# Laying K, V, dK and dV out in DRAM so that each partition moves 8 KB in one run instead of 4 KB twice

## The chip, the cores and the metric

The kernel runs on one core of one Trainium2 chip. The metric is the time of one execution on the device in microseconds. Executions of the kernel before in one round agree within 0.3 to 1% (691.9 to 694.2 us in one, 690.6 to 697.3 in another), and a ratio is called faster or slower only beyond 2%. The rearrangement of the arrays on the host is not in the time.

## The reference

Attention with grouped heads, forward and backward, in bf16. There are 32 batches; in each, 32 query heads of 4 rows share 4 K/V heads of 2048 rows, with 128 columns.

```python
def _fwd_reference(q, k, v):               # q (32, 32, 4, 128); k, v (32, 4, 2048, 128)
    k = jnp.repeat(k, rep, axis=1)         # rep = 8
    v = jnp.repeat(v, rep, axis=1)
    p = _softmax(jnp.einsum("bhqd,bhkd->bhqk", q, k) * D ** -0.5, axis=-1)
    return jnp.einsum("bhqk,bhkd->bhqd", p, v)

def reference(q, k, v, grad_out):          # returns out, dq, dk, dv
    _out, _vjp = jax.vjp(_f, q, k, v)
    return (_out, *_vjp(grad_out))
```

The 128 query rows of a batch fill the 128 partitions. K, V, dK and dV of a batch are 2 MB each, 8 MB together. The other four arrays come to 128 KB per batch.

## The kernel before

K and V come in as pairs of heads, 1 MB per transfer. On each of the 128 partitions lie 16 rows of one head (4 KB, contiguous in DRAM) and 16 rows of the other (4 KB, 512 KB away). dK and dV leave in the same form. A batch therefore has eight transfers of 1 MB on the sync engine's queue (SP) and four of 32 KB on GpSimd's (POOL). TensorE transposes K and V (L372 in the profile), transposes the softmax and its gradient (L431), and does the products (L383, L442, L477). ScalarE (ACT) and VectorE (DVE) empty PSUM. The order of all instructions over the batches is fixed by a table.

```python
CAP = dict(q=4, k=8, v=4, ..., out=6)      # buffers; a K or V buffer holds one pair of heads
...
pairs = lambda t: t.rearrange("b (g h) (p c) d -> b g p h (c d)", c=C, h=2)
k_r, v_r, dk_r, dv_r = pairs(k), pairs(v), pairs(out_2), pairs(out_3)
...
elif name in ("LK", "LV"):                                          # L358
    g, = arg
    p_, src = (k_pool, k_r) if name == "LK" else (v_pool, v_r)
    x = p_.tile([P, 2, C, D], BF16, name="k_sb" if name == "LK" else "v_sb")
    whole = x[:].rearrange("p h c d -> p h (c d)")
    for h in range(2) if b == 0 else [slice(0, 2)]:
        nc.sync.dma_start(out=whole[:, h], in_=src[b, g][:, h])
...
elif name in ("DVs", "DKs"):                                        # L492
    g, = arg
    nc.sync.dma_start(out=(dv_r if name == "DVs" else dk_r)[b, g],
                      in_=t[name[:2], "out", g][:].rearrange("p h c d -> p h (c d)"))
```

Eight K buffers are four batches, four V buffers are two. Each 1 MB transfer has one of eight completion semaphores in turn, so at most eight are in flight.

Of the kernel before, what the change touches and what calls it, by code (L numbers as in the profile page):

```python
# [15 lines left out]
P = 128  # L16
NH = 4
# [261 lines left out]
def kernel(  # L279
# [10 lines left out]
):  # L290
    nc = tc.nc
    B, Hq, Sq, D = q.shape
    Hkv, Sk = k.shape[1], k.shape[2]
    assert D == P and Hq * Sq == P and Hkv == NH and Hq // Hkv * Sq == 32
    C = Sk // P
    QW = Sk // NQ
# [16 lines left out]
    make_identity(nc, ident[:])  # L313

    rows = lambda t: t.rearrange("b h s d -> b (h s) d")
    pairs = lambda t: t.rearrange("b (g h) (p c) d -> b g p h (c d)", c=C, h=2)
    q_r, go_r, o_r, dq_r = rows(q), rows(grad_out), rows(out_0), rows(out_1)
    k_r, v_r, dk_r, dv_r = pairs(k), pairs(v), pairs(out_2), pairs(out_3)

# [178 lines left out]
                emit(u)  # L498

_INS = ['q', 'k', 'v', 'grad_out']  # L500
_OUTS = [((32, 32, 4, 128), 'bfloat16'), ((32, 32, 4, 128), 'bfloat16'), ((32, 4, 2048, 128), 'bfloat16'), ((32, 4, 2048, 128), 'bfloat16')]

# [23 lines left out]
```

## Time and profile before

| | before |
|---|---|
| time, median | 692.5 us (691.9 to 694.2, 4 runs) |
| span of the profiled execution | 688.6 us |
| TensorE, ScalarE busy | 90%, 88% |
| packets on the main queue | 70,784 |

Lines of the page of the kernel before: the rate of the transfers in 40 slices of the span, the queues, and the chain of work that ended last.

```profile
GB/s 347 403 413 387 415 414 409 415 415 416 415 416 416 414 416 412 397 407 413 408 409 405 410 412 414 399 398 412 405 412 405 406 401 397 408 403 386 391 260 263
...
q1 hardware_dynamic: 70784, 268.45, 97.6%
q0 software_dynamic: 4096, 4.20, 1.8%
q8 instruction: 96, 1.57, 0.8%
...
DMA 55%; PE 22%; ACT 13%; issue 5%; POOL 3%; DVE 2%; SPq 0%; POOLq 0%; DVEq 0%; ACTq 0%
```

Queue q1 carries the 1 MB transfers, q0 the small ones, q8 the instructions of TensorE. The rate is about 415 GB/s until slice 16 (280 us) and about 405 after it. More than half of the chain is transfers.

The busy time of the engines in three stretches of the kernel before (columns: stretch in us, its length, then busy us and number of instructions for TensorE, its weight loads, VectorE, ScalarE and GpSimd, then granted clock, share of the transfer engines, GB/s):

```profile
100.00:270.00 170.00, 160.65 (x3237) 121.44 (x3233) 143.79 (x200) 159.04 (x242) 55.71 (x112) 1.00 1.03 415
300.00:380.00 80.00, 73.68 (x1470) 55.96 (x1467) 65.64 (x91) 72.62 (x111) 26.12 (x52) 1.00 1.02 408
400.00:600.00 200.00, 182.26 (x3626) 136.86 (x3624) 162.23 (x230) 179.46 (x274) 59.05 (x119) 1.00 1.02 406
```

TensorE is busy 94.5% of the first stretch and 91 to 92% of the others. The waits of the kernel before from 270 to 600 us (total, number, longest) say why:

```profile
PEld L372 <- DMA v_sb<-in_v_dram: 18.4, 15, 1.5
PE psum L372 <- DMA v_sb<-in_v_dram: 11.3, 14, 1.0
```

TensorE waits for V here, and for no load between 100 and 270 us. One pace follows from the starts of the exponentials: 20.3 us per batch from batch 5 to batch 12, and 21.14 from batch 14 to batch 28.

### The profile page before, as it was taken

The page shows a single profiled execution, that of the slowest core. Times are in us where ns is not written, and L with a number is a line of the kernel's source. Part 1 is how long each engine was busy: PE and PEld are TensorE (multiplying, and loading weights), DVE is VectorE, ACT ScalarE, POOL GpSimd, SP SyncE. Part 2 cuts the span into 40 slices and gives each one's busy share as a digit, 9 for nine tenths or more (in the row PEclk, how much of TensorE's full clock was granted, in tenths as well). Part 3 has the DMA queues.
Part 4 walks back from the last instruction along what each step waited for, and adds up shares of the span by engine and source line. Part 5 has one row for each costly group of instructions (what it writes and reads, how often), then busy time and mean ns, then how long its engine had stood idle before and what let it go on. Part 6 is the DMA issues. An engine that isn't in the chain of part 4 may idle for free.

```text
span 688.6 us, 28403 instructions
## 1 busy us (share of the span) xinstructions
PE 620.1 (90%) x12352; PEld 467.1 (68%) x12352; DVE 558.3 (81%) x776; ACT 604.4 (88%) x921; POOL 208.8 (30%) x426
## 2 busy tenths in 40 slices
PE   5899999999999999999999899998889998989984
PEld 4677677777677777766667666676666766766753
DVE  3788888888889888888788878787787887888885
ACT  2889999999999999998899888899888998888883
POOL 2423321333322233331233321333212333113330
PEclk9999999999999999999999999999999999999998
DMA  9999999999999999999999999999999999999967
GB/s 347 403 413 387 415 414 409 415 415 416 415 416 416 414 416 412 397 407 413 408 409 405 410 412 414 399 398 412 405 412 405 406 401 397 408 403 386 391 260 263
DMA packets 75005, 274.47 MB, mean 399 GB/s; under 512 B 6272, under 2 KB 6272, under 8 KB 74880
## 3 DMA queue, kind: packets, MB, share of 16 engines
q1 hardware_dynamic: 70784, 268.45, 97.6%
q0 software_dynamic: 4096, 4.20, 1.8%
q8 instruction: 96, 1.57, 0.8%
q14 instruction: 29, 0.24, 0.1%
HBM read 136.31 MB, written 136.31 MB: 396 GB/s over the span
## 4 chain that ended last, share of the span: by engine, by line
DMA 55%; PE 22%; ACT 13%; issue 5%; POOL 3%; DVE 2%; SPq 0%; POOLq 0%; DVEq 0%; ACTq 0%
DMA v_sb<-in_v_dram 52%; PE psum L372 10%; PE psum L477 6%; ACT dk_sb L483 4%; ACT dv_sb L483 4%; PE psum L431 3%; DMA out_dram<-dv_sb 2%; ACT e_sb L399 2%; PE psum L442 2%; ACT vt_sb L337 2%; POOL dop_sb_103 L411 1%; PE psum L383 1%; DVE kt_sb L390 1%; ACT kt_sb L337 1%; DMA go_sb<-in_grad_out_dram 1%
## 5 line engine op out<-in xcount | busy, mean ns | idle before, releaser
L483 ACT CAST dk_sb<-psum 128x1024 bf16<-128x1024 f32 x159 | 157.6, 1013 | 25.9 <-PE psum L477 24.5
L483 ACT CAST dv_sb<-psum 128x1024 bf16<-128x1024 f32 x155 | 151.7, 1022 | 13.2 <-PE psum L477 12.4
L372 PE MATMUL psum<-ident,v_sb 128*128 128x128 bf16 x2048 | 147.4, 220 | 16.8 <-DMA v_sb<-in_v_dram 15.3
L372 PEld LDWEIGHTS <-v_sb 128*128 128x128 bf16 x2048 | 117.9, 98 | 56.9 <-issue 32.8
L372 PE MATMUL psum<-ident,k_sb 128*128 128x128 bf16 x2048 | 142.4, 221 | 10.2 <-ACT dk_sb L483 10.2
L372 PEld LDWEIGHTS <-k_sb 128*128 128x128 bf16 x2048 | 121.4, 99 | 27.1 <-issue 24.3
L483 DVE CAST dv_sb<-psum 128x1024 bf16<-128x1024 f32 x101 | 122.8, 1220 | 10.8 <-PE psum L477 10.6
L483 DVE CAST dk_sb<-psum 128x1024 bf16<-128x1024 f32 x97 | 115.9, 1219 | 8.5 <-ACT kt_sb L337 4.5
L337 ACT COPY kt_sb<-psum 128x512 f32<-128x512 f32 x190 | 110.3, 595 | 6.6 <-PE psum L372 5.1
L411 POOL TENSOR_SCALAR dop_sb_103<-go_sb,rinv 32x128 bf16<-32x128 bf16 x64 | 38.5, 602 | 225.4 <-DVE rinv L404 97.3
L411 POOL TENSOR_SCALAR dop_sb_102<-go_sb,rinv 32x128 bf16<-32x128 bf16 x64 | 38.5, 602 | 212.5 <-DVE rinv L404 141.1
L463 DVE SCALAR_TENSOR_TENSOR ds_sb<-psum,delta,e_sb 128x1024 bf16<-128x1024 f32 x64 | 81.9, 1279 | 15.1 <-ACT vt_sb L337 13.5
L337 ACT COPY vt_sb<-psum 128x512 f32<-128x512 f32 x131 | 75.5, 599 | 17.6 <-PE psum L372 16.6
L340 DVE COPY vt_sb<-psum 128x1024 bf16<-128x1024 bf16 x125 | 82.9, 681 | 2.9 <-PE psum L372 2.6
L477 PEld LDWEIGHTS <-e_sb 64*128 64x128 bf16 x1024 | 50.0, 93 | 36.3 <-issue 19.6
L399 ACT ACTIVATE e_sb<-psum,m 128x1024 bf16<-128x1024 f32 x64 | 71.1, 1122 | 2.4 <-DVE kt_sb L390 2.2
L340 DVE COPY kt_sb<-psum 128x1024 bf16<-128x1024 bf16 x66 | 44.9, 685 | 18.8 <-PE psum L372 18.8
L477 PEld LDWEIGHTS <-ds_sb 64*128 64x128 bf16 x1024 | 43.3, 94 | 23.8 <-issue 8.8
L477 PE MATMUL psum<-dop_sb_103,e_sb 64*128 64x256 bf16 x512 | 45.2, 270 | 4.1 <-POOL dop_sb_103 L411 1.6
L477 PE MATMUL psum<-dop_sb_102,e_sb 64*128 64x256 bf16 x512 | 44.9, 270 | 3.2 <-ACT dv_sb L483 0.7
L390 DVE TENSOR_SCALAR_CACHE_REDUCE kt_sb<-psum 128x1024 bf16<-128x1024 f32 x32 | 39.2, 1225 | 9.6 <-issue 7.7
L390 DVE TENSOR_SCALAR_CACHE_REDUCE kt_sb<-psum,m 128x1024 bf16<-128x1024 f32 x32 | 41.1, 1284 | 6.5 <-DVE kt_sb L390 3.9
(83 smaller groups left out, 764.5 us busy)
## 6 DMA issues: line engine op xcount, KB each, us to landing
k_sb<-in_k_dram SPq DMA_DIRECT2D x62, 1024.0 KB, 18.7
v_sb<-in_v_dram SPq DMA_DIRECT2D x62, 1024.0 KB, 19.6
out_dram<-dv_sb SPq DMA_DIRECT2D x62, 1024.0 KB, 19.0
out_dram<-dk_sb SPq DMA_DIRECT2D x62, 1024.0 KB, 18.8
k_sb<-in_k_dram SPq DMA_DIRECT2D x4, 512.0 KB, 5.4
v_sb<-in_v_dram SPq DMA_DIRECT2D x4, 512.0 KB, 9.4
out_dram<-dv_sb SPq DMA_DIRECT2D x4, 512.0 KB, 7.9
out_dram<-dk_sb SPq DMA_DIRECT2D x4, 512.0 KB, 6.7
```

Source lines behind the costliest of these rows:

```text
L337: nc.scalar.copy(out=out.rearrange("p c d -> p (c d)").bitcast(FP32), in_=in_.rearrange("p c d -> p (c d)").bitcast(FP32))
L340: nc.vector.tensor_copy(out=out, in_=in_)
L372: nc.tensor.transpose(out=ps[:, j, :], in_=t[x, h][:, 8 * i + j, :], identity=ident[:])
L383: nc.tensor.matmul(t[name, i][r, QW * w:QW * w + QW], lhsT=t["qdt"][:, side, r], rhs=t[x, h, i][:, CPQ * w:CPQ * w + CPQ, :], start=True, ...
L390: nc.vector.tensor_scalar(out=spent, in0=t["S", i][:], scalar1=-scale, scalar2=t["m"][:] if i else None, op0=ALU.mult, op1=ALU.min, accum_ ...
L399: nc.scalar.activation(out=t["e"][:, 2 * QW * i:2 * QW * i + 2 * QW], in_=t["S", i][:], func=ACT.Exp, bias=t["m"][:], scale=scale, accum_o ...
L411: nc.gpsimd.tensor_scalar(out=t["dop"][r, h % 2, :], in0=t["go"][r, :], scalar1=t["rinv"][r, :], scalar2=None, op0=ALU.mult)
L431: nc.tensor.transpose(out=ps[:, j, :], in_=src[:, P * c:P * c + P], identity=ident[:])
L442: nc.tensor.matmul(t[name][r, 0:D], lhsT=t[xt, c // 8][:, c % 8, r], rhs=t[x, h][:, c, :], start=(c == 0), stop=(c == C - 1), tile_positio ...
L463: nc.vector.scalar_tensor_tensor(out=t["ds"][:, w], in0=t["DP", i][:], scalar=t["dl"][:], in1=t["e"][:, w], op0=ALU.subtract, op1=ALU.mult)
L477: nc.tensor.matmul(accs[g][:, 2 * P * j:2 * P * j + 2 * P], lhsT=t[lhs][r, P * c:P * c + P], rhs=t[rhs][r, :, :].rearrange("p h d -> p (h ...
L483: copy(out=t[name[:2], "out", g][:, :, CPQ * i:CPQ * i + CPQ, :], in_=t[name[:2], i][g][:].rearrange("p (c h d) -> p h c d", h=2, d=D))
```

## The change

The host lays K and V out as (batch, pair, partition, head, 16 rows, column) and undoes it for dK and dV, so each partition's 8 KB is one contiguous run in DRAM. The intent is half as many packets for the same bytes. No instruction of the compute engines changes.

```diff
-    Hkv, Sk = k.shape[1], k.shape[2]
+    Hkv, Sk = k.shape[1] * k.shape[3], k.shape[2] * k.shape[4]
...
-    pairs = lambda t: t.rearrange("b (g h) (p c) d -> b g p h (c d)", c=C, h=2)
+    pairs = lambda t: t.rearrange("b g p h c d -> b g p h (c d)")
...
-_OUTS = [..., ((32, 4, 2048, 128), 'bfloat16'), ((32, 4, 2048, 128), 'bfloat16')]
+_OUTS = [..., ((32, 2, 128, 2, 16, 128), 'bfloat16'), ((32, 2, 128, 2, 16, 128), 'bfloat16')]
+
+def paired(x):
+
+    return x.reshape(32, 2, 2, P, 16, P).transpose(0, 1, 3, 2, 4, 5)
+
+def unpaired(x):
+    return x.transpose(0, 1, 3, 2, 4, 5).reshape(32, NH, 16 * P, P)
...
-        a = _np.ascontiguousarray(inputs[name])
+        a = _np.ascontiguousarray(paired(_np.asarray(inputs[name])) if name in "kv" else inputs[name])
...
-    return got
+    return got[:2] + tuple(unpaired(_np.asarray(x)) for x in got[2:])
```

More of the change, by code (lines that the diff above doesn't have):

```diff
@@ L500 @@
 _INS = ['q', 'k', 'v', 'grad_out']
-_OUTS = [((32, 32, 4, 128), 'bfloat16'), ((32, 32, 4, 128), 'bfloat16'), ((32, 4, 2048, 128), 'bfloat16'), ((32, 4, 2048, 128), 'bfloat16')]
+_OUTS = [((32, 32, 4, 128), 'bfloat16'), ((32, 32, 4, 128), 'bfloat16'), ((32, 2, 128, 2, 16, 128), 'bfloat16'), ((32, 2, 128, 2, 16, 128), 'bfloat16')]
+def paired(x):
+    return x.reshape(32, 2, 2, P, 16, P).transpose(0, 1, 3, 2, 4, 5)
+def unpaired(x):
+    return x.transpose(0, 1, 3, 2, 4, 5).reshape(32, NH, 16 * P, P)
 def kernel(**inputs):
```

## The prediction

> **What bounds the kernel now.** Two stretches.
>
> 1. About 55 to 280 us: compute. The starts of the exponentials advance by 20.35 us per batch (116.6 to 259.0 us, 7 batches). TensorE's waits name no load; it is busy 94.5%, ScalarE 93%.
> 2. About 280 to 600 us: transfers. The step becomes 21.14 us (299.8 to 595.8 us, 14 batches). TensorE falls to 91%; the waits name v_sb landing (PE 11.3 us, weight loads 18.4 us). The chain that ended last is v_sb loads there (52% of the span).
>
> The transfer engines are full in both (share 1.02 to 1.03 in the table by stretch). Stretch 1 draws on K tiles loaded ahead; transfers deliver a batch every 20.67 us by my sum. When the lead is gone, stretch 2 begins.
>
> **What changes.** PE, ACT, DVE and POOL instructions stay, and so do order and bytes of the sync engine's queue. Its 1 MB transfers become 128 rows of 8 KB instead of 256 of 4 KB. The 512 KB transfers of the first and last batch keep 4 KB and 2 KB rows.
>
> From the trace's packet records: 64512 packets of 4096 B, median 159 ns; 2048 B take 84 to 86 ns. So a packet costs about 9 ns plus 75 per 2 KB, hence 309 for 8 KB, which the few 8192 B packets on the system's queue do have. That would save 2.8%. But packets overlap: they sum to 51.3 us per engine in 50 us, some 4.2 ns per packet. The pitch is then about 155 ns, and 305 for 8 KB (estimates): 1.6%. The Trainium skill, "DMA: Bandwidth & Descriptors", section "Why small descriptors are slow (HBM only)", states a fixed cost of about 3 cycles per packet on 32-byte beats; at the 850 MHz of its section "Where 436 GB/s comes from" that is an estimate of 154 and 305 ns, which agrees with this trace's 155.
>
> Per batch (2048 packets become 1024, over 16 engines) 19.8 us becomes 19.5: 0.3 us saved.
>
> **On the critical path.** In stretch 1 nothing. In stretch 2 a batch takes 21.1 us, and 20.75 after, if the slow packets remain (excess 1.0 to 1.7 us per 50 us there, 0.4 to 0.7 in stretch 1). But stretch 1 drains its lead by 20.67 − 20.35 = 0.3 us per batch, and the change saves just that: the lead may never run out, and 20.35 us holds to the end. That saves 14 × 0.79 = 11 us. If the slow packets return, 14 × 0.3 = 4 us plus a later onset make 6. I take 9.
>
> **Prediction: 684.0 us, range 678.0 to 690.0.** Faster by over 2% 0.11, within 2% 0.86, slower by over 2% 0.03. The compute pace caps the gain near 2%.
>
> **What the profile would show.**
> - Main queue's packets near 39,000 (from 70,784), mostly 8 KB, median near 309 ns; if they stay 4 KB, no gain.
> - Rate in the middle 415 to 422 GB/s instead of 405 to 410.
> - Step per batch after 280 us at 20.3 to 20.8 us; TensorE's waits on v_sb below 15 us.
> - Chain shifted from v_sb loads to TensorE and ScalarE.
>
> **What would make it wrong.** Longer packets stalling more (a median above 318 ns, twice 159, removes the gain); the new DRAM addresses colliding; the small queue waiting behind 8 KB packets; or compute not being limited at 20.35 us, which would allow over 2%.

## The result, and the profile after

The changed kernel took 687.45 us (686.57 to 688.13, 4 runs) against 692.54 before, 5.1 us less. The ratio is 0.9925, with a 95% interval of 0.9907 to 0.9943: within 2%, but clear of noise. Ratios are the mean time of one kernel's fast runs over that of the other's of the same rounds, so not quite the ratio of the medians quoted here.

The same lines of the page of the changed kernel:

```profile
GB/s 338 417 413 384 424 418 412 418 416 414 418 417 412 420 416 420 417 422 413 419 422 420 416 419 416 410 412 396 423 410 411 409 375 411 409 381 390 348 252 255
...
q1 hardware_dynamic: 39040, 268.45, 95.7%
q0 software_dynamic: 4096, 4.20, 1.9%
q8 instruction: 96, 1.57, 0.8%
...
DMA 41%; PE 27%; ACT 18%; issue 7%; POOL 3%; DVE 2%; POOLq 0%; ACTq 0%; DVEq 0%; SPq 0%
```

The packets are nearly halved. Their records in the trace say that an 8192 B packet takes 309 ns (median), where a 4096 B packet took 159, and that a packet on the same engine starts 3 ns (8192 B) or mostly 4 ns (4096 B) before the end of the one ahead. The pitch, from the start of one packet to the start of the next, is therefore 305.9 ns against 2 x 155.3 = 310.6, which is 1.5% less. Yet the rate falls again, from slice 25 (about 430 us) instead of slice 16, and the chain still holds 41% of transfers.

The same stretches and waits of the changed kernel, and what its sync engine waited for:

```profile
100.00:270.00 170.00, 159.85 (x3221) 120.83 (x3221) 143.03 (x200) 157.89 (x241) 55.16 (x112) 1.00 1.01 416
300.00:380.00 80.00, 75.16 (x1522) 57.15 (x1521) 68.07 (x97) 75.00 (x115) 26.01 (x52) 1.00 1.01 419
400.00:600.00 200.00, 183.11 (x3656) 137.68 (x3653) 163.51 (x230) 180.77 (x277) 62.14 (x126) 1.00 1.00 408
```

```profile
PEld L372 <- DMA v_sb<-in_v_dram: 12.6, 11, 1.7
PE psum L372 <- DMA v_sb<-in_v_dram: 7.3, 10, 1.2
```

```profile
SPq L358 <- DMA v_sb<-in_v_dram: 51.3, 27, 2.7
SPq L358 <- DMA k_sb<-in_k_dram: 47.6, 25, 2.8
...
SPq L492 <- DMA out_dram<-dv_sb: 37.9, 25, 2.7
```

In the middle stretch the rate rose from 408 to 419 GB/s and TensorE went from 92 to 94% busy. After 400 us little changed: 408 GB/s instead of 406. So the time came from a later onset of the slow stretch. Batches 14 to 18 now start 20.37 us apart, 0.8 us closer. From batch 18 to 28 the mean step is 21.04 us, where the kernel before has 21.15 over the same batches (the medians are 20.94 and 21.14; two of the ten steps took 21.6 us after, one before). The sums agree: 4 x 0.8 + 10 x 0.1 = 4.2 us, less 0.8 us that batches 5 to 12 lost (20.45 us per step instead of 20.35), is 3.4; by the starts of batches 5 and 28 it is 3.7. (The profiled execution of before happened to be one of the quick ones, so the two spans differ by 3.0 us only. The onset is read from one profile of each kernel: in e8 and e10 below, the changed kernel with one tiny load more per batch from batch 14 on, the slow stretch begins at batch 15 or 16.)

The sync engine's waits on landed transfers are almost new: from 270 to 600 us, where these are counted too, they come to 1.8 us in the kernel before, all for V loads. One view shows where it stood before: the instructions that issue the V loads (minimum, median and maximum ns of one), in the kernel before and then in the changed one.

```profile
L358 SPq DMA_DIRECT2D v_sb<-in_v_dram x66: 368/1115/5424, 2.6 to 638.1; - x66
```

```profile
L358 SPq DMA_DIRECT2D v_sb<-in_v_dram x66: 327/340/1250, 2.7 to 634.8; - x66
```

Before, with twice as many descriptors, the issue itself was held up (2.4 us in the median of all transfers of the queue from 300 to 600 us, with seven in flight). Now the issue is quick (0.34 us), and it is the transfer eight places earlier that must land first. In both kernels the queue is full and the limit lies behind it.

What lies behind it shows in the completion records. Each 1 MB transfer raises its semaphore 16 times. The Trainium skill, "DMA: Bandwidth & Descriptors", section "Why a DMA increments its semaphore by 16 and not by 1", explains this: each of the 16 engines adds one when its own share has landed. The times of the 16 increments are in the trace. Here they are for one V load of each kernel, in us after issue (worked out from the trace):

```
before, issued at 402.7 us:  7.4  7.6  7.8  8.0  8.5  8.5  9.0  9.3  9.3  9.6 10.9 10.9 11.1 11.6 12.6  19.6
after,  issued at 398.4 us:  5.8  5.8  5.8  6.2  6.2  6.4  7.4  9.8  9.9 10.6 10.9 11.5 11.6 12.3 12.4  20.9
```

Fifteen engines are done in 13 us, one takes 20. At 100 us all were done within about 5 us of one another in both kernels. One engine falls behind until the others have run as far ahead as the queue lets them, and from then on its pace is the pace of all transfers. Its time per transfer, from one last landing to the next between 400 and 600 us (medians), is 2.50 us for a load and 2.71 us for a store before, 2.47 and 2.71 after. Its packets at the pitch alone would take 2.49 us (16 x 155.3 ns, and 6 ns for the 4-byte packet that raises the semaphore) before and 2.45 (8 x 305.9 + 6) after. So its loads take little more than that, and its stores 0.2 us or more. By array the medians fell a little each: dV from 2.82 to 2.79 us, dK from 2.70 to 2.67, K from 2.49 to 2.46, V from 2.53 to 2.51.

The question for the runs was: is the packet cost as computed, why is one engine slow on stores, and does that limit the kernel? My theory was that the transfers by themselves gain 0.3 us per batch, and that something belonging to the compute side slows one engine. The rivals: the transfers as such have a slow engine, the small transfers of GpSimd cause it, or the traffic of ScalarE and VectorE to SBUF does.

### The profile page after: what moved, and what is told of

The parts are those of the page before. It is cut to its first block, busy times and chain, and to the rows that moved or that the text cites. A ratio compares the mean times of both kernels' runs of the same rounds, so it can differ in the third digit from the quotient of the medians.

```text
span 685.6 us, 28403 instructions
## 1 busy us (share of the span) xinstructions
PE 619.8 (90%) x12352; PEld 467.5 (68%) x12352; DVE 558.4 (81%) x776; ACT 603.8 (88%) x921; POOL 207.9 (30%) x426
## 3 DMA queue, kind: packets, MB, share of 16 engines
q1 hardware_dynamic: 39040, 268.45, 95.7%
q0 software_dynamic: 4096, 4.20, 1.9%
## 4 chain that ended last, share of the span: by engine, by line
DMA 41%; PE 27%; ACT 18%; issue 7%; POOL 3%; DVE 2%; POOLq 0%; ACTq 0%; DVEq 0%; SPq 0%
DMA v_sb<-in_v_dram 37%; PE psum L372 12%; PE psum L477 7%; ACT dk_sb L483 6%; ACT dv_sb L483 5%; PE psum L431 4%; DMA out_dram<-dv_sb 4%; ACT e_sb L399 3%; PE psum L442 2%; ACT vt_sb L337 2%; POOL dop_sb L411 2%; ACT kt_sb L337 2%; PE psum L383 1%; DMA go_sb<-in_grad_out_dram 1%; DVE kt_sb L390 1%
## 5 line engine op out<-in xcount | busy, mean ns | idle before, releaser
L411 POOL TENSOR_SCALAR dop_sb<-go_sb,rinv 32x128 bf16<-32x128 bf16 x128 | 76.8, 600 | 435.5 <-DVE rinv L404 182.9
L477 PE MATMUL psum<-dop_sb,e_sb 64*128 64x256 bf16 x1024 | 89.9, 270 | 7.0 <-POOL dop_sb L411 2.0
L477 PE MATMUL psum<-qp_sb,ds_sb 64*128 64x256 bf16 x1024 | 81.1, 271 | 2.3 <-DVE ds_sb L463 0.8
L419 POOL TENSOR_SCALAR qp_sb<-q_sb,rinv 32x128 bf16<-32x128 bf16 x128 | 50.0, 391 | 10.3
L431 PE MATMUL psum<-ident,ds_sb 128*128 128x128 bf16 x512 | 38.7, 219 | 8.6 <-ACT e_sb L399 8.6
```

The source lines that it names most:

```text
L411: nc.gpsimd.tensor_scalar(out=t["dop"][r, h % 2, :], in0=t["go"][r, :], scalar1=t["rinv"][r, :], scalar2=None, op0=ALU.mult)
L419: nc.gpsimd.tensor_scalar(out=t["qp"][r, h % 2, :], in0=t["q"][r, :], scalar1=t["rinv"][r, :], scalar2=scale, op0=ALU.mult, op1=ALU.mult)
L431: nc.tensor.transpose(out=ps[:, j, :], in_=src[:, P * c:P * c + P], identity=ident[:])
L477: nc.tensor.matmul(accs[g][:, 2 * P * j:2 * P * j + 2 * P], lhsT=t[lhs][r, P * c:P * c + P], rhs=t[rhs][r, :, :].rearrange("p h d -> p (h ...
```

## The experiments

All were made from the two kernels by small edits. Those marked wrong give wrong results. Where there is a single run (e5, e6, e8, e9, e10), only differences far larger than the noise are used. In all tables "lag" is how long after the next slowest engine the slowest one lands, and store and load are the slowest engine's times per 1 MB; all three are medians between 400 and 600 us, worked out from the completion records.

| run | store | load | lag |
|---|---|---|---|
| before | 2.71 us | 2.50 us | 7.8 us |
| after | 2.71 | 2.47 | 9.8 |
| e1, transfers alone, 4 KB | 2.47 | 2.52 | 0.4 |
| e2, transfers alone, 8 KB | 2.43 | 2.47 | 1.1 |
| e3, no small transfers | 2.68 | 2.46 | 8.6 |
| e5, e2 + 386 TensorE transposes per batch | 2.68 | 2.47 | 8.1 |
| e6, e2 + ScalarE and VectorE copies | 2.47 | 2.46 | 1.0 |
| e9, e2 + 96 wide TensorE matmuls per batch | 2.51 | 2.46 | 3.2 |

### e1 and e2: transfers alone (wrong)

All computation is taken out of the kernel before (e1) and of the changed one (e2). What was loaded is stored two batches later. V has eight buffers instead of four there (cut here), so that loads can run ahead.

```diff
-        for u in order:
-            if u.on or not u.eng:
-                emit(u)
+        for b in range(B + 2):
+            if b < B:
+                ...   # q, grad_out on GpSimd's queue; K and V pairs on the sync queue
+            if b >= 2:
+                ...   # dV <- V, dK <- K of batch b-2 on the sync queue; out, dq on GpSimd's
```

> All computation taken out of the kernel before; the same loads and stores in 4 KB rows, and the same small transfers, remain (results wrong on purpose). What it tells apart: in both kernels one of the 16 transfer engines completes its share of each 1 MB transfer 8 to 10 us after the next slowest one, and on it a store takes about 2.70 us against 2.49 for a load. If that slow engine belongs to the transfers themselves: it lags here too, about 20.9 us per batch, 675 us in all. If the compute engines, their instruction fetches or their semaphores cause it: no lag, 8 x 2.54 = 20.3 us per batch, 655 us.

> As the run before, with 8 KB rows. Fixed cost per packet (each packet starts 3 ns before the end of the one ahead, so 156 ns per 4 KB, 306 per 8 KB): 2.49 us per 1 MB becomes 2.455, 0.28 us per batch, 9 us less than the run with 4 KB rows, whichever engine limits. If the slow engine loses time per byte on stores, it gains less: 4 to 7 us. Rival, that longer rows stall more at DRAM: no gain or a loss.

Measured: e1 662.69 us, e2 653.30 us (four runs each, within 1.4 us). The lines for the rate and the main queue, e1 first:

```profile
GB/s 332 393 404 398 394 404 408 420 420 421 420 420 420 420 420 421 420 420 420 420 420 421 420 420 420 420 420 421 420 420 420 420 421 421 420 420 420 420 421 313
...
q1 hardware_dynamic: 69632, 268.45, 99.7%
```

```profile
GB/s 343 401 410 411 401 410 413 426 422 427 426 422 425 427 427 425 427 426 427 428 428 428 427 428 428 427 427 428 428 428 427 427 428 428 427 428 428 428 427 298
...
q1 hardware_dynamic: 36864, 268.45, 98.3%
```

Between the two only the rows differ. From 200 to 600 us the rate goes from 420 to 427 GB/s, 1.7%, of which the pitch of the packets gives 1.5. The 9.4 us between the runs (9 were expected) are 0.29 us per batch: the gain that the prediction computed exists. No engine lags here. The slow engine does not belong to the transfers as such. A time of 655 us was expected for e1 without a slow engine, 675 with one; 663 lies between, and it is the lag that decides.

### e3: no small transfers (wrong)

```diff
-            t["q"] = sm_pool.tile([P, D], BF16, name="q_sb")
-            nc.gpsimd.dma_start(out=t["q"][:], in_=q_r[b])
-            ...                                             # the same for grad_out
+            if b == 0:
+                ...                                         # load q and grad_out of batch 0 once
+            t["q"], t["go"] = T[0]["q"], T[0]["go"]
...
-            nc.gpsimd.dma_start(out=(o_r if name == "Os" else dq_r)[b], in_=...)
+            if b == B - 1:
+                nc.gpsimd.dma_start(out=(o_r if name == "Os" else dq_r)[b], in_=...)
```

> The changed kernel without the small transfers of the GpSimd queue, except the first batch's loads and the last batch's stores (results wrong on purpose). If the small transfers make one engine slow: no engine lags, no wait on v_sb, 20.35 us per batch to the end, 677 us. If that engine is slow on the big stores: it loses only the small packets' own time, about 0.4 us per batch, still lags by 5 us or more late in the run, its stores still take 0.2 us longer than its loads, steps of 20.4 to 20.6 us late, 679 to 683 us.

Measured: 678.75 us, ratio to the kernel before 0.9785 (0.9734 to 0.9835). Steps are 20.4 us from batch 14 to 28. The waits on V from 270 to 600 us, in e3:

```profile
PEld L373 <- DMA v_sb<-in_v_dram: 4.7, 6, 1.9
PE psum L373 <- DMA v_sb<-in_v_dram: 1.6, 2, 1.4
```

The engine still lags, by 8.6 us, and its stores still take 2.68 us. The small transfers do not make it slow. But they take their share of its time, and without them it nearly keeps pace with compute: 8.7 us less than the changed kernel by the medians, from different rounds (in which the kernel before had 694.0 and 692.5 us). Leaving them out relieves all 16 engines, so the time alone does not single out the slow one; the lag does.

### e4: half of the stores (wrong)

```diff
+            if g == 0:
                 nc.sync.dma_start(out=(dv_r if name == "DVs" else dk_r)[b, g], ...)
```

> The changed kernel with half of the dV and dK stores left out, so a quarter of the bytes less (results wrong on purpose). If compute's pace is 20.35 us per batch as in the early stretch: 20.35 to the end, no wait on v_sb, 673 to 678 us, and no more to be had from transfers. If compute itself is slowed by the transfers, or is faster than that: steps below 20.2 us and under 670 us.

Measured: 672.75 us, ratio 0.9695 (0.9653 to 0.9736). The same three stretches, in e4:

```profile
100.00:270.00 170.00, 161.10 (x3249) 122.18 (x3249) 144.25 (x201) 159.70 (x244) 55.03 (x111) 1.00 0.85 319
300.00:380.00 80.00, 76.06 (x1536) 57.55 (x1534) 67.83 (x96) 74.89 (x115) 26.02 (x52) 1.00 0.85 317
400.00:600.00 200.00, 189.09 (x3802) 143.63 (x3803) 169.66 (x237) 187.31 (x286) 62.96 (x127) 1.00 0.85 318
```

With the transfer engines at 85%, TensorE stays at 94.5 to 95% to the end. Steps are 20.24 us from batch 5 to 12 and 20.27 from 18 to 28, with no wait of TensorE on V from 270 to 600 us. This is compute's own pace, a little under the 20.35 us of the prediction. It puts the floor for any transfer change of this kernel near 673 us. It does not tell the slow engine from all 16 together, since all have less to do.

### e5, e6 and e9: what slows the one engine (wrong)

To e2 were added, per batch and tied to no transfer: 386 small transposes on TensorE (e5), 18 ScalarE and 16 VectorE copies from PSUM to SBUF (e6), or 96 TensorE matmuls of 512 columns, as busy with a quarter of the instructions (e9).

```diff
         for b in range(B + 2):
+            if b < B:
+                for n in range(386):                                            # e5
+                    nc.tensor.transpose(out=psum[...], in_=ident[:], identity=ident[:])
+                for n in range(18):                                             # e6
+                    nc.scalar.copy(out=wa[0][:], in_=psum[:, 0:1024])
+                for n in range(16):
+                    nc.vector.tensor_copy(out=wa[1][:], in_=psum[:, 2048:3072])
+                for n in range(96):                                             # e9
+                    nc.tensor.matmul(psum[...], lhsT=ident[:], rhs=wide[:], start=True, stop=True)
```

> The 8 KB transfers alone, which ran at 2.44 us per store and 2.47 per load with no engine far behind, plus 386 TensorE transposes per batch on a constant tile, tied to nothing (results wrong on purpose). If TensorE's instruction stream, which comes through the transfer engines, is what slows one engine in the real kernel: instruction packets of 16 KB appear, stores reach 2.65 us or more on one engine, which falls behind by 5 us or more, and the run takes 10 to 25 us more than 653. If ACT, DVE or SBUF traffic is the cause: only some 0.2 us per batch for the instruction packets, under 662 us, no single engine behind.

> The 8 KB transfers alone plus 18 ACT copies and 16 DVE copies per batch from PSUM to SBUF, tied to no transfer (results wrong on purpose). If SBUF or PSUM traffic of ACT and DVE slows one transfer engine: stores 2.65 us or more, a single engine 5 us or more behind, 663 us or more. If TensorE's instruction stream does: as without them, 651 to 655 us.

> The 8 KB transfers alone plus TensorE work that keeps it as busy as before (96 matmuls of 512 columns per batch) with a quarter of the instructions (results wrong on purpose). With 386 small transposes per batch the stores took 2.68 us late on the slow engine and it fell 11 us behind. If the instruction stream does it: about a quarter of the instruction packets (some 24), stores at 2.50 us or less on average late, lag of 3 us or less. If TensorE's activity itself does it (its reads of SBUF, power, clock): stores at 2.65 us or more and a lag of 8 us or more as before.

Measured, one run each: e5 696.47 us, e6 655.23 us, e9 670.10 us. The times of e5 and e9 are TensorE's own, so the last landing is what to compare: 675.9 us in e5 and 655.6 in e9, against 650.6 in e2 and 652.5 in e6. The line of busy engines and the instruction packets, e5 first, then e9, and the busy engines of e6:

```profile
PE 691.4 (100%) x12352; PEld 691.1 (99%) x12352; POOL 69.7 (10%) x134
...
q8 instruction: 96, 1.57, 0.8%
```

```profile
PE 665.0 (100%) x3072; PEld 301.0 (45%) x3072; DVE 0.3 (0%) x1; POOL 69.8 (10%) x134
...
q8 instruction: 24, 0.39, 0.2%
```

```profile
DVE 630.2 (96%) x513; ACT 584.2 (89%) x577; POOL 69.8 (11%) x134
```

TensorE's work alone makes a slow engine: in e5 stores of 2.68 us on it, 8 us of lag (11 at most), and landings 25 us later than in e2. With TensorE 100% busy on a quarter of the instructions (e9), the stores lose 0.08 us instead of 0.25 over those of e2, and the end moves by 5 us instead of 25; both the stores and the lag of 3.2 us lie just above what was expected of the instruction stream (2.50 and 3). ScalarE and VectorE do nothing of the kind. So it is not how busy TensorE is. Not tested apart is the loading of weights, which fills 99% of e5 and 45% of e9. In the changed kernel it fills 68%, with as many instructions as in e5 and stores as slow, which speaks for the number of instructions. That the slow engine of e5 is the same one as in the kernel was not probed.

What it is about an instruction of TensorE, the packet records narrow down. The fetches are the 96 packets of 16 KB, each some 950 ns. In e5, 23 of the 39 stores between 400 and 600 us saw no fetch on any engine for more than 0.3 us, and they took 2.68 us all the same. On the slow engine, the packets of 19 of the 39 stores can be followed one by one, from the 3 or 4 ns by which they overlap: they take 333 ns in the median (eight in ten 333 to 347) instead of 309, with no fetch between them, while its load packets take 309. So each store packet is slowed a little, and it is not the fetches' own time. Whether it is the record that the profile keeps of every instruction, these runs do not show. As far as the record tells, no run was made without the profiler, so whether the kernel has a slow engine without it is open too. So is why only stores suffer, and only on one engine. In the changed kernel the two dK stores of a batch lose 0.1 to 0.3 us each on the slow engine, mostly with no instruction packet under way in that time.

### e7: 16 KB rows, transfers alone (wrong)

```diff
-    pairs = lambda t: t.rearrange("b g p h c d -> b g p h (c d)")
+    pairs = lambda t: t.rearrange("b p h c d -> b p (h c d)")          # all four heads side by side
...
-                        nc.sync.dma_start(out=t[x, g][:]..., in_=src[b, g])
+                        nc.sync.dma_start(out=t[x][64 * g:64 * g + 64], in_=src[b][64 * g:64 * g + 64])
```

> Transfers alone in 16 KB rows (64 rows per 1 MB, all four heads side by side; results wrong on purpose). Fixed cost per packet: 2.455 us per 1 MB becomes 2.43, 0.14 us per batch, 4 to 5 us less than 653: 648 us, with packets of 16 KB. Rival, that the gain ends at 8 KB because packets are cut there or stall more: 652 to 656 us or more.

Measured: 711.58 and 720.91 us in two runs; two more, 767.33 and 777.97 us, are over 1.5% above the fastest (the clock is the same in all four). The profiled run was the quickest. Its rate and main queue:

```profile
GB/s 187 223 211 281 252 350 355 377 404 392 399 401 406 410 415 413 409 407 410 413 414 416 426 418 420 419 420 420 420 421 423 426 415 416 415 415 417 417 431 283
...
q1 hardware_dynamic: 20480, 268.45, 97.5%
```

The expectation missed. The packets are of 16 KB, 611 ns in the median, as the fixed cost says; but their mean is 674 ns, and in the first 140 us the rate is 187 to 377 GB/s. Late stores take 2.42 us as expected, late loads 2.57. So there is no gain past 8 KB in this form, and the rate from 400 to 600 us is 420 GB/s where e2 has 427. This run also changes which partitions one transfer covers (64 instead of 128), so the row length is not shown to be the cause.

### e8 and e10: which engine is slow

One tiny extra load per batch from batch 14 on, of n rows, beside the first dV store.

```diff
         elif name in ("DVs", "DKs"):
             g, = arg
+            if name == "DVs" and g == 0 and b >= 14:
+                n = (15, 14, 12, 8, 4, 2, 1, 15, 8)[(b - 14) % 9]               # e10: (7, 6, 5)[b % 3]
+                nc.sync.dma_start(out=probe[n][0:n, :], in_=q_r[b][0:n, 0:32])
```

> The changed kernel with one tiny extra load on the sync queue per batch from batch 14 on, of 15, 14, 12, 8, 4, 2 or 1 rows. [...] With one engine 7 to 10 us behind: where the load includes it, some 19 to 21 us to landing, where not, 8 to 13 us. The smallest count that lands late brackets the slow engine. If 15 rows land early it is the highest one. Time 686 to 692 us.

> Probes of 7, 6 and 5 rows in place of the earlier counts, which put the slow engine among the fifth to the eighth of the 16: loads of 8 rows or more landed after 18.3 us, of 4 rows or fewer after 5.6 us or less (one 6.6). If it is the eighth: 7 rows land within 5 to 10 us. If it is the fifth: 5 rows take over 18 us too. Time 686 to 692 us.

By the section of the Trainium skill named above, a load whose outer dimension is n (15 or less) uses the n lowest-numbered engines, and the sequencer adds what is missing to 16 at once. The trace agrees on the count: one increment after 0.5 us and n later ones, after 3 us or more. Last landings in us after issue, all but the last probe of each run (that one came when the queue was draining), worked out from the trace:

```
rows    15          14          12          8                 4         2         1
e8      18.4 18.2 18.3   18.3 18.3   18.3 18.5   18.3 18.3 19.0   5.6 6.6   5.6 5.3   6.2 6.3
rows    7                       6                         5
e10     18.2 18.3 18.2 18.4 19.2   18.3 18.4 18.4 18.5 19.0   18.5 18.3 18.9 18.4 19.2 19.1
```

Five rows or more land late, four or fewer early (and sooner than the 8 to 13 us expected): it is the fifth of the 16 engines, given that numbering, which no run here shows. In the probes that land late, exactly one increment is late; the others came within 12 us. Both runs are correct and took 689.0 and 688.6 us. The expectation of e10 that it might be the eighth missed, and its other half, the fifth, held.

### e11 and e12: giving rows to the slow engine, or taking them from it

```diff
+            cut = (0, 112, 117, 122, 127, 128) if name == "LK" and g == 0 and b % 2 and b < B - 1 else (0, P)
+            #     (0, 112, 116, 120, 124, 128) in e12
             for h in range(2) if b == 0 else [slice(0, 2)]:
-                nc.sync.dma_start(out=whole[:, h], in_=src[b, g][:, h])
+                for r0, r1 in zip(cut, cut[1:]):
+                    nc.sync.dma_start(out=whole[r0:r1, h], in_=src[b, g][r0:r1, h])
```

> The changed kernel with one K load of every second batch cut into 112 rows, three times 5 rows and 1 row. The probes say that the slow engine is the fifth; it then gets 10 rows of that load instead of 8, like the second to fourth. If that engine sets the pace late in the run: 0.61 us per second batch more, 0.3 us per batch, steps of about 21.2 us instead of 20.9 in the late stretch, which starts earlier: 692 to 697 us against 687.5. If the pace is set by all engines together or by something else: no change beyond 1 us, 686 to 689 us.

> As the run before, same bytes and as many transfers, but the rows are cut into 112 and four times 4, so the fifth engine gets 7 rows instead of 8 and the first four get 11. If the fifth engine sets the pace: 0.3 us per second batch less, steps of 20.7 to 20.9 us, 684 to 688 us, and 6 us or more below the run with 5 rows. If the cutting itself costs time (more transfers, fewer bytes in flight): both runs alike, over 689 us.

Measured: e11 718.66 us, ratio 1.0371 (1.0338 to 1.0404); e12 722.93 us, ratio 1.0429 (1.0396 to 1.0461). Both are correct. Both are far slower than the changed kernel, and the one that relieves the fifth engine is no faster (the two intervals overlap a little). This is the outcome "the cutting itself costs", and it was larger than I allowed for. The mean 8 KB packet took 332 ns in e11 and 335 in e12, where the changed kernel had 318. The pair does not test what it was built for, and why the cut makes packets slower is open.

## Why the prediction was right, and where it was off

- **Time.** 687.45 us lies in the range of 678 to 690, and "within 2%" was given 0.86. The gain is 5.1 us where 8.5 was the centre. Of the two cases in the prediction, the one with "a later onset" and 6 us in all is near what happened; the other, 11 us, did not come. But its terms came out the other way round: it had 4 us from quicker batches in the slow stretch and 2 from the later onset, and the trace has about 1 and 3. That the sum is near is partly luck.
- **Packets.** 39,040 packets, 309 ns in the median: both as predicted. The pitch is right as well: 155.3 and 305.9 ns, where 155 and 305 were predicted. Transfers alone gained 1.4% in time (e1 against e2), where the packets were predicted to gain 1.6%.
- **Compute's pace as the cap.** Right. e4 shows it at 20.24 to 20.27 us per batch, against 20.35 predicted, and 673 us in all.
- **Rate and step.** 415 to 422 GB/s and 20.3 to 20.8 us per batch were predicted for the middle. It is 419 GB/s between 300 and 380 us, but 408 from 400 to 600; 20.37 us up to batch 18, but 21.04 after it.
- **Waits and chain.** TensorE's own waits on V fell to 7.3 us, but with its weight loads they are 19.9 from 270 to 600 us. The chain moved only partly, from 55 to 41% of transfers.
- **The step that was off**: "In stretch 2 a batch takes 21.1 us, and 20.75 after, if the slow packets remain". Once stretch 2 has begun, a batch takes 21.04 us instead of 21.15 in the mean, and 20.94 instead of 21.14 in the median: 0.1 to 0.2 us saved, not 0.35. The prediction divided all packets by 16 engines and spread the slow ones evenly. In the trace one engine sets the pace in that stretch, and a store takes it 0.2 us or more longer than the packet pitch gives, before and after. By the medians its eight transfers of a batch gained 0.2 us together, of the 0.3 that the pitch gives. The mean gained less because of single long steps; why, two profiles do not show.
- **"The lead may never run out"** failed because of the rate at which the lead drains. The prediction had transfers deliver a batch every 20.67 us, a sum over 16 engines, only 0.3 us behind compute. The slow engine needs 21.15 us, 0.8 behind, so a saving of 0.3 us at most could not hold the lead. In transfers alone the 16 engines stay within 6 us of each other late in e2; in the changed kernel the fifth falls behind from about 200 us on, and the lead of K and V runs out four batches later than before instead of never.

What is shown: the packet cost, the single slow engine, and that TensorE's work alone produces one, less of it with fewer instructions. That this engine limits the kernel is read from the landings, where fifteen shares are in long before the last; e3 and e4 fit, but relieve all 16 engines alike. What is only argued: that the number of instructions matters rather than the loading of weights, and that relieving the fifth engine without cutting transfers would bring the kernel to about 673 us. No correct version tried here beats the changed kernel.

## What to carry to other kernels

When transfers are the limit, look at the 16 completions of single transfers before dividing bytes by 16: here the slowest engine set the pace, and whether a saving is enough has to be asked of that one. A change that speeds transfers by x% moves such a kernel only through the stretch that waits on them, and here even that mostly by postponing its onset. Measure the transfers alone and compute with fewer bytes first: two runs gave both floors, 653 and 673 us.

## What the Trainium skill lacked or had wrong

- "DMA: Bandwidth & Descriptors", section "Latency and other measured facts", says that engines 7 and 15 (counted from 0) are usually the slow ones and suspects the descriptor rings of GpSimd's transfers (SWDGE). Here it was the fifth of the 16, number 4 (e8, e10), and an engine stayed slow without those transfers (e3, lag 8.6 us).
- No page has it that a busy TensorE slows one transfer engine's stores, and more so with many instructions: 2.68 us per 1 MB instead of 2.43 with 386 instruction pairs per batch, 2.51 with 96 (e5, e9).
- "DMA: Bandwidth & Descriptors", section "Why small descriptors are slow (HBM only)": the estimate from a fixed cost of about 3 cycles per packet, 154 and 305 ns, is 1 ns below the measured pitch of 155.3 and 305.9; the same estimate with 4 cycles gives both. The page does not say that the packet records overlap by 3 to 4 ns, so that their durations alone overstate the cost (159 and 309 ns).
- "Perfetto Trace Analysis", section "DMA Optimizations", advises batching to 4 or 8 KB because larger is better. In transfers alone, 4 to 8 KB gained 1.4% of the time (e1, e2); 16 KB rows in 64-row transfers lost, 712 and 721 us against 653 (e7), which the page does not warn of.
- "HBM Reference", section "Specifications (TRN2)", gives about 425 GB/s for a core streaming alone and does not say whether stores are among it. With 8 KB rows, loads and stores mixed, the run agrees: 427 GB/s (e2).
- No page has a number for how long the issue of a transfer is held up when many descriptors wait: with 4 KB rows and seven 1 MB transfers in flight the issuing instruction took 2.4 us in the median, with 8 KB rows 0.34.
